# Layer B's phi on a copy: one evacuation of PSUM for the projections that need phi, and phi without a relu

## The chip, the cores and the metric

The kernel runs on one core of a Trainium2 chip. The metric is the device time of one execution in microseconds (us). The kernel before was timed in 3 runs. A profiled execution gives the trace; its times start at the beginning of its span.

Five engines work side by side, each through its own queue in order: PE (TensorE, matmuls and transposes into PSUM), PEld (its weight loads), DVE (VectorE), ACT (ScalarE), POOL (GpSimd), and SP, which issues transfers.

## What is computed

Four layers are applied one after the other to x of 2048 rows and 640 columns, in the order A, B, A, B, each as x + layer(layernorm(x)). There are 32 heads of 20 columns. Layer A is linear attention. Layer B cuts the rows into N = 4 segments of L = 512 and adds a memory, made of the keys of the segments before, to causal softmax attention inside a segment:

```python
phi = lambda t: jnp.where(t > 0, t + 1.0, jnp.exp(t))
for s in range(N):
    qs, ks, vs = q[:, :, s], k[:, :, s], v[:, :, s]
    logits = jnp.einsum("bhqd,bhkd->bhqk", qs, ks) * scale + mask
    p = _softmax(logits, axis=-1)
    a_dot = jnp.einsum("bhqk,bhkd->bhqd", p, vs)
    pq = phi(qs)
    num = jnp.einsum("bhld,bhde->bhle", pq, M)
    den = jnp.einsum("bhld,bhd->bhl", pq, z)[..., None] + 1e-6
    o = g * (num / den) + (1.0 - g) * a_dot
    outs.append(o)
    pk = phi(ks)
    M = M + jnp.einsum("bhld,bhle->bhde", pk, vs)
    z = z + jnp.einsum("bhld->bhd", pk)
```

So the queries need phi from segment 1 on (in segment 0 the memory is empty), and the keys need it up to segment 2 (nothing reads the memory after segment 3).

## The kernel before

**Projections of layer B.** `b_project` runs once for each segment. It makes v first, and then, for t = 0 to 4, a tile of 128 rows of the transposed queries and one of the transposed keys, each 128 x 512, with `proj_t`: 15 matmuls (L391) on pairs of fp16 halves into one PSUM bank of 512 fp32 columns. There are eight banks, handed out in turn by `bank`. The weights were scaled by a power of two, so a projection is p times `inv`, one value per partition.

Each such bank has up to three uses. `split_store` makes its fp16 half (L830, ScalarE) and the rest that the half leaves (L831, VectorE) in the tile `nat` of two buffers, and sends both to DRAM (`qd`, `kd`) with two transfers on SP's queue (L834, L835 for queries, L837, L838 for keys). Where phi is wanted, `phi` then takes the exponential (L428) and the relu (L430) of the same bank on ScalarE, both scaled by `inv`, into two buffers of the tag `er`, and VectorE makes min(exp, 1) + relu of them (L431). For queries that goes to `pq`, which `read_mem` multiplies with the memory (L457) once the next stretch of layer A runs; for keys to `pkT`, of one buffer, which `pk_turn` transposes on PE (L858) after the next query projection, ScalarE evacuates (L860, `pkt`) and `update` multiplies with v (L868, added to `acc` at L872 or L874).

**Attention of layer B** goes through head groups: four heads each, eight groups a segment. `stacks` loads their rows of `qd` and `kd` into `qs` and `ks` (L979, SP's queue); `row_max` makes scores (L993) and their row maxima with VectorE (L999); `max_rows` turns the maxima (L1017, L1019) and sends them into `qs` (L1022); `scores` makes the transposed scores (L1034), their exponential with ScalarE (`pe`, L1038) and masks the diagonal blocks with GpSimd (L1045); `weigh` multiplies with v (L1061); `evacuate` (L1067) and `normalize` (L1074 to L1085) write the result to `otok`.

**Order.** PE's order is written out by hand: `run` steps two streams in turn by planned costs. One is `dense` (layer A, projections, output products), the other `attend` (attention of the segment before). So while segment 1 to 3 is projected, the attention of the segment before runs, and in segment 3 of the first layer B and after it the output products follow. Inside `dense`, the projections of segment s are woven with the output of segment s - 2 and the head of layer A's next segment (`p_read`, L754 to L760). In segment 0 the projections run without attention; the second half of layer A (`a_second`, L483, `moments`) for segment 1 follows. The order of the other engines is made by the framework's scheduler, which moves instructions by their dependencies; the waits between engines are put in by it.

**Opening.** The first run through layer A also prepares all weights: it finds their maxima, the scales `scl` and their inverses `inv` (L259 to L264), and splits the weights (L269, L270). `last`, inside `opening`, ends it with `scales("B")` and the gates.

## Time and profile before

| | us |
|---|---|
| median of 3 runs | 1704.46 |
| lowest and highest | 1704.25, 1706.57 |
| profiled execution | 1704.55 |
| its span | 1702.8 |
| mean granted clock of TensorE in it | 0.992 |

The projections of queries and keys in layer B run at 299 to 337, 398 to 463, 539 to 618 and 695 to 766 us in the first layer B, and at 1129 to 1167, 1228 to 1293, 1365 to 1428 and 1498 to 1555 us in the second, for segments 0 to 3.

A row of the profile's groups gives line, engine, operation, output and inputs by the program's names, shapes and the count; behind the bars stand the busy time in us and the mean ns of one, and the idle time of that engine just before, with what ended it. In the timeline and the chain of waits each row starts with its start and its duration in us.

### The profile page before, as it was taken

The page shows a single profiled execution, that of the slowest core. Times are in us where ns is not written, and L with a number is a line of the kernel's source. Part 1 is how long each engine was busy: PE and PEld are TensorE (multiplying, and loading weights), DVE is VectorE, ACT ScalarE, POOL GpSimd, SP SyncE. Part 2 cuts the span into 40 slices and gives each one's busy share as a digit, 9 for nine tenths or more (in the row PEclk, how much of TensorE's full clock was granted, in tenths as well). Part 3 has the DMA queues.
Part 4 walks back from the last instruction along what each step waited for, and adds up shares of the span by engine and source line. Part 5 has one row for each costly group of instructions (what it writes and reads, how often), then busy time and mean ns, then how long its engine had stood idle before and what let it go on. Part 6 is the DMA issues. An engine that isn't in the chain of part 4 may idle for free.

```text
span 1702.8 us, 37843 instructions
## 1 busy us (share of the span) xinstructions
PE 1637.9 (96%) x13788; PEld 1018.6 (60%) x13788; DVE 1272.3 (75%) x4015; ACT 994.2 (58%) x1888; POOL 505.9 (30%) x1046
## 2 busy tenths in 40 slices
PE   7999979999999999999999999999999999999998
PEld 5767757554465556556566777765546545645555
DVE  7888887487887788759874465847888978878773
ACT  6666533347756746667776454333675676666673
POOL 3442222013223322333452210310322332233452
PEclk9999989999999999999999999999999999999999
DMA  6424654421322331353211303423232323323432
GB/s 218 151 75 169 223 203 152 136 98 59 111 79 69 115 118 56 128 183 95 72 56 39 117 32 125 178 94 123 70 110 89 114 83 110 102 86 111 140 103 95
DMA packets 110372, 191.00 MB, mean 112 GB/s; under 512 B 14172, under 2 KB 69596, under 8 KB 107624
## 3 DMA queue, kind: packets, MB, share of 16 engines
q1 hardware_dynamic: 97704, 142.68, 25.9%
q0 software_dynamic: 3264, 24.91, 4.1%
q10 hardware_dynamic: 9216, 20.98, 3.2%
q8 instruction: 109, 1.79, 0.4%
q14 instruction: 79, 0.65, 0.1%
HBM read 109.32 MB, written 78.64 MB: 110 GB/s over the span
## 4 chain that ended last, share of the span: by engine, by line
PE 66%; DVE 17%; ACT 9%; issue 3%; DMA 3%; POOL 2%; SPq 0%; ACTq 0%; POOLq 0%; DVEq 0%
PE ps L406 25%; PE ps L391 13%; PE ps L1061 8%; PE ps L580 4%; PE ps L1034 4%; ACT pe L1038 3%; PE ps L993 3%; PE ps L329 3%; DVE ps L999 3%; PE ps L457 2%; PE ps L1074 1%; DVE e L421 1%; DVE wmx L243 1%; DVE split L270 1%; DVE xT L334 1%
## 5 line engine op out<-in xcount | busy, mean ns | idle before, releaser
L999 DVE CUSTOM_DVE_ANT_0 ps<-ps,maskw 128x512 f32<-128x512 f32 (+3 forms) x1024 | 472.0, 518 | 28.7 <-PE ps L993 25.9
L1038 ACT ACTIVATE pe<-ps,lsc 128x512 f32<-128x512 f32 x640 | 395.4, 696 | 63.0 <-PE ps L1034 59.8
L406 PEld LDWEIGHTS <-xT 128*128 128x128 f16 x2880 | 282.2, 99 | 115.0 <-issue 6.2
L1045 POOL TENSOR_SCALAR_AFFINE_SELECT pe<-pe 128x256 f32<-128x256 f32 (+1 forms) x640 | 233.4, 372 | 350.5 <-ACT pe L1038 342.7
L406 PEld LDWEIGHTS <-oT 128*128 128x128 f16 x1920 | 184.5, 98 | 84.7 <-issue 8.3
L1061 PE MATMUL ps<-pe,v 128*32 128x512 f32 (+3 forms) x2048 | 161.6, 436 | 8.8 <-DVE oT L334 1.9
L406 PE MATMUL ps<-wm,oT 128*128 128x320 f16 x960 | 141.3, 299 | 3.8 <-DVE rs L352 2.6
L406 PE MATMUL ps<-w_Bo,oT 128*128 128x320 f16 x960 | 141.5, 299 | 3.2 <-ACT oT L333 2.0
L406 PE MATMUL ps<-w_Ak,xT 128*128 128x320 f16 x960 | 140.6, 303 | 3.1 <-DVE xT L334 1.0
L406 PE MATMUL ps<-w_Bv,xT 128*128 128x320 f16 x960 | 142.3, 303 | 0.2
L391 PE MATMUL ps<-xT,w_Bq 128*128 128x512 f16 x600 | 140.9, 379 | 1.3 <-ACT pe L1038 0.8
L999 DVE DVE_READ_ACCUMULATOR2_ANT mg<- 128x1 f32 x1024 | 142.1, 139 | 0.1
L580 PE MATMUL ps<-pk,xs 128*128 128x321 f16 (+1 forms) x960 | 140.7, 304 | 1.1 <-DVE pk L543 0.7
L391 PE MATMUL ps<-xT,w_Bk 128*128 128x512 f16 x600 | 138.5, 379 | 1.2 <-ACT pe L1038 1.2
L406 PE MATMUL ps<-w_Aq,xT 128*128 128x320 f16 x960 | 137.6, 299 | 0.1
L993 PE MATMUL ps<-ks,qs 60*128 60x512 f16 (+3 forms) x1024 | 123.5, 297 | 7.6 <-ACT pe L1038 3.5
L580 PEld LDWEIGHTS <-xs 128*128 128x128 f16 x960 | 93.9, 99 | 41.0 <-issue 1.6
L421 DVE SCALAR_TENSOR_TENSOR e<-e,r 128x320 f32<-128x320 f32 x128 | 69.6, 544 | 53.6 <-ACT r L420 53.0
L1034 PE MATMUL ps<-qs,ks 62*128 62x512 f16 (+3 forms) x1024 | 105.6, 300 | 2.1 <-ACT pe L1038 1.1
L1061 PEld LDWEIGHTS ps<-pe,v 128*32 128x32 f32 x2048 | 65.4, 109 | 68.7 <-issue 40.9
L831 DVE SCALAR_TENSOR_TENSOR nat<-ps,nat 128x512 f16<-128x512 f32 x80 | 55.2, 690 | 62.6 <-ACT nat L830 62.3
L391 PEld LDWEIGHTS <-w_Bk 128*128 128x128 f16 x600 | 57.1, 98 | 66.5 <-issue 6.4
(202 smaller groups left out, 2359.6 us busy)
## 6 DMA issues: line engine op xcount, KB each, us to landing
x<-xn ACTq DMA_DIRECT2D x48, 320.0 KB
qs<-qd SPq DMA_DIRECT2D x128, 120.0 KB
ks<-kd SPq DMA_DIRECT2D x128, 120.0 KB
xo<-x SPq DMA_DIRECT2D x48, 320.0 KB
pqi<-pqd SPq DMA_DIRECT2D x32, 320.0 KB
qd<-nat SPq DMA_DIRECT2D x40, 256.0 KB
kd<-nat SPq DMA_DIRECT2D x40, 256.0 KB
x<-in_A_x SPq DMA_DIRECT2D x16, 320.0 KB
```

The source lines that it names most:

```text
L329: nc.tensor.transpose(pt[:, (c - c0) * P:(c - c0 + 1) * P], src[:, c * P:(c + 1) * P], self.ident)
L391: nc.tensor.matmul(p, w[:, c, a, t * P:(t + 1) * P], xT[:, c, b, :], start=k == 0, stop=k == 3 * C - 1)
L406: nc.tensor.matmul(p, xT[:, c, a, i * P:(i + 1) * P], w[:, c, b, n * HN:(n + 1) * HN], start=k == 0, stop=k == 3 * C - 1)
L421: nc.vector.scalar_tensor_tensor(e, e, 1.0, r, op0=OP.min, op1=OP.add)
L580: nc.tensor.matmul(p, xs[:, i, a, c * P:(c + 1) * P], pk[i][:, b, cols], start=i == 0 and a == b, stop=i == NT - 1 and a == 1)
L831: nc.vector.scalar_tensor_tensor(nat[:, 1], p, QK_SHIFT, nat[:, 0], op0=OP.mult, op1=OP.subtract)
L993: nc.tensor.matmul(bs[par][:, a:a + n], qs[r, p, i * P:(i + 1) * P], ks[r, p, :n], start=True, stop=True)
L999: nc.vector.tensor_tensor_reduce(bs[par][:, a:a + n], bs[par][:, a:a + n], self.maskw[:, SEG - n:], 1.0, NEG, OP.add, OP.max, G["mg"][:, p ...
L1034: nc.tensor.matmul(b[:, a:a + n], ks[r, p, j * P:(j + 1) * P], qs[r, p, j * P:], start=True, stop=True)
L1038: nc.scalar.activation(e, b, AF.Exp, scale=self.lsc)
L1045: nc.gpsimd.affine_select(d, d, pattern=pat, compare_op=OP.is_ge, fill=0.0, base=0, channel_multiplier=-1)
L1061: nc.tensor.matmul(G["pv"][32 * h4:32 * h4 + 32, j * P:], v[j][:, h * E1:h * E1 + 32], G.pop((p, par, j)), start=j == 0, stop=j == 2, skip ...
```

## The change

For projections that need phi, `split_store` gets the tile that phi is to fill (`dst`: pq or pkT). ScalarE first copies the bank, scaled by `inv`, into that tile. The fp16 half, its rest and the exponential then read the copy. Since the copy is already scaled, the shift of the fp16 half becomes a value per partition, `nat_scl`, the shift times `scl`; it is made in `last`, for queries and keys. phi is then taken in place: VectorE takes min(exp, 1) in SBUF, in an instruction of its own, and then the larger of copy + 1 and that. There is no relu, and `phi` is gone. Projections that need no phi (queries of segment 0, keys of segment 3) go through `split_store` as before. In `b_project` the tile is taken ahead of `split_store`.

```diff
-    def phi(self, p, inv, dst):
-        nc, sb = self.nc, self.sb
-        n = p.shape[-1]
-        e = sb.tile([P, 512], F32, tag="er", name="e", bufs=3)[:, :n]
-        nc.scalar.activation(e, p, AF.Exp, scale=inv)
-        r = sb.tile([P, 512], F32, tag="er", name="r", bufs=3)[:, :n]
-        nc.scalar.activation(r, p, AF.Relu, scale=inv)
-        nc.vector.scalar_tensor_tensor(dst, e, 1.0, r, op0=OP.min, op1=OP.add)
...
-    def split_store(self, p, dd, t, key):
+    def split_store(self, p, dd, t, key, dst=None):
         nc = self.nc
         nat = self.bp.tile([P, 2, SEG], F16, tag="nat", name="nat", bufs=2)
-        nc.scalar.activation(nat[:, 0], p, AF.Copy, scale=QK_SHIFT)
-        nc.vector.scalar_tensor_tensor(nat[:, 1], p, QK_SHIFT, nat[:, 0], op0=OP.mult, op1=OP.subtract)
+        shift = QK_SHIFT
+        if dst is not None:
+            shift = self.nat_scl[key]
+            nc.scalar.activation(dst, p, AF.Copy, scale=self.inv["B", key])
+            p = dst
+        nc.scalar.activation(nat[:, 0], p, AF.Copy, scale=shift)
+        nc.vector.scalar_tensor_tensor(nat[:, 1], p, shift, nat[:, 0], op0=OP.mult, op1=OP.subtract)
+        if dst is not None:
+            e = self.sb.tile([P, SEG], F32, tag="er", name="e", bufs=3)
+            nc.scalar.activation(e, dst, AF.Exp)
+            nc.vector.tensor_scalar(e, e, 1.0, None, op0=OP.min)
+            nc.vector.scalar_tensor_tensor(dst, dst, 1.0, e, op0=OP.add, op1=OP.max)
...
             p = yield from self.proj_t(xT, w["q"], t)
-            self.split_store(p, st["qd"], t, "q")
+            pq = None
             if s > 0:
                 pq = sb.tile([P, SEG], F32, tag="pq", name="pq", bufs=PQ)
-                self.phi(p, self.inv["B", "q"], pq)
                 st["pq"].append(pq)
+            self.split_store(p, st["qd"], t, "q", pq)
...
             p = yield from self.proj_t(xT, w["k"], t)
-            self.split_store(p, st["kd"], t, "k")
             if s < NSEG - 1:
                 pkT = bp.tile([P, SEG], F32, tag="pkT", name="pkT", bufs=1)
-                self.phi(p, self.inv["B", "k"], pkT)
+            self.split_store(p, st["kd"], t, "k", pkT)
...
             self.scales("B")
+            self.nat_scl = {}
+            for n in "qk":
+                self.nat_scl[n] = self.cp.tile([P, 1], F32, name="nat_scl" + n)
+                self.nc.vector.tensor_scalar(self.nat_scl[n], self.scl["B", n], QK_SHIFT, None, op0=OP.mult)
```

## The prediction

> **What bounds the kernel now.** First the page: span, busy shares, and the shares by engine of the chain of waits.
>
> ```profile
> span 1702.8 us, 37843 instructions
> ...
> PE 1637.9 (96%) x13788; PEld 1018.6 (60%) x13788; DVE 1272.3 (75%) x4015; ACT 994.2 (58%) x1888; POOL 505.9 (30%) x1046
> ...
> PE 66%; DVE 17%; ACT 9%; issue 3%; DMA 3%; POOL 2%; SPq 0%; ACTq 0%; POOLq 0%; DVEq 0%
> ```
>
> TensorE sets most of the time. VectorE is 75% busy but is the link that ended last for only 17%. The profiled execution took 1704.55 us for a span of 1702.8, 0.09 above the median of 1704.46; the sum below is made on 1704.55.
>
> Then the table of busy time, in the stretches where layer B's projections run: segment 0 of the first layer B, then its segments 1 to 3, then segments 1 to 3 of the second. The columns are length, PE, PEld, DVE, ACT, POOL, clock, DMA.
>
> ```profile
> 299.00:337.00 38.00, 37.76 (x302) 18.75 (x300) 13.90 (x27) 14.00 (x25) 1.27 (x1) 1.00 0.42 137
> 398.00:463.00 65.00, 62.83 (x579) 29.73 (x579) 53.01 (x195) 50.39 (x90) 19.13 (x49) 1.00 0.29 96
> 539.00:618.40 79.40, 74.58 (x625) 39.19 (x627) 59.28 (x191) 49.68 (x90) 30.20 (x55) 1.00 0.37 119
> 695.00:765.70 70.70, 69.14 (x501) 35.76 (x500) 45.46 (x161) 45.28 (x80) 25.19 (x54) 1.00 0.48 154
> ...
> 1228.00:1293.00 65.00, 62.55 (x567) 29.53 (x571) 52.94 (x195) 50.27 (x90) 18.89 (x49) 1.00 0.29 96
> 1365.00:1428.00 63.00, 60.88 (x563) 29.12 (x566) 52.38 (x186) 48.37 (x86) 20.93 (x49) 1.00 0.31 100
> 1498.00:1555.00 57.00, 55.70 (x428) 25.20 (x427) 44.41 (x168) 40.52 (x71) 19.02 (x48) 1.00 0.30 97
> ```
>
> PE idles 0.2 us of the first stretch and 2.2, 4.8, 1.6, 2.5, 2.1 and 1.3 us of the others: 14.5 us in all. A gain here can hardly pass that. VectorE already has 53 of 65 us in segment 1, so a loss has more room.
>
> Third, one key projection of segment 0 in the timeline (start, duration, engine, line; idle before it and its releaser in brackets).
>
> ```profile
> 305.91 0.60 ACT L830 ACTIVATE nat<-ps 128x512 f16<-128x512 f32 x1 [2.64 <-PE ps L391]
> ...
> 306.54 0.69 DVE L831 SCALAR_TENSOR_TENSOR nat<-ps,nat 128x512 f16<-128x512 f32 x1 [2.54 <-ACT nat L830]
> ...
> 307.26 0.69 ACT L428 ACTIVATE e<-ps,inv_Bk 128x512 f32<-128x512 f32 x1 [0.76 <-DVE nat L831]
> ...
> 307.85 0.68 ACT L430 ACTIVATE r<-ps,inv_Bk 128x512 f32<-128x512 f32 x1
> 308.56 0.69 DVE L431 SCALAR_TENSOR_TENSOR pkT<-e,r 128x512 f32<-128x512 f32 x1 [1.33 <-ACT r L430]
> ...
> 309.35 0.63 PE L858 MATMUL ps<-ident,pkT 128*128 128x128 f32 x4 [0.24 <-PE ps L391]
> ```
>
> The exponential reads the PSUM bank that L831 reads, and starts 0.03 us after L831 ends, though it uses nothing that L831 makes. ScalarE stands idle 0.76 us for it, and the bank is held 2.6 us, until the relu ends at 308.53. Over the kernel:
>
> ```profile
> L831 DVE SCALAR_TENSOR_TENSOR nat<-ps,nat x80: 676/691/694, 303.3 to 1555.7; 128x512 f16<-128x512 f32 x80
> ...
> ACT e L428: 20.2, 28
> ```
>
> Fourth, the chain of waits by line, in segment 1 and segment 2 of the first layer, and in segments 1 and 3 of the second.
>
> ```profile
> by line: PE ps L391 38.5%; PE ps L1061 14.3%; PE ps L993 7.2%; ACT pe L1038 7.0%; PE ps L1034 5.3%; DMA pqi<-pqd 5.2%; issue 2.9%; PE ps L868 2.3%; DVE nat L831 2.1%; ACT e L428 2.1%; PE ps L1074 2.0%; ACT r L430 1.8%; ACT nat L830 1.7%; SP
> by line: PE ps L391 21.0%; PE ps L406 11.3%; PE ps L1061 9.2%; issue 6.8%; ACT pe L1038 5.5%; PE ps L1034 4.3%; DVE nat L831 4.2%; PE ps L993 3.4%; DVE pqi L754 3.2%; ACT e L428 2.7%; ACT r L430 2.6%; POOL xn L481 2.6%; PE ps L1074 2.2%; DV
> by line: PE ps L391 38.5%; PE ps L1061 14.3%; ACT pe L1038 7.0%; PE ps L993 6.9%; DMA pqi<-pqd 5.7%; PE ps L1034 5.3%; issue 2.8%; PE ps L868 2.3%; DVE nat L831 2.1%; ACT e L428 2.1%; PE ps L1074 2.0%; ACT r L430 1.8%; ACT nat L830 1.7%; DV
> by line: PE ps L391 56.9%; PE ps L1061 12.1%; PE ps L1034 8.7%; PE ps L993 7.4%; DVE ps L999 6.2%; PE ps L1074 2.3%; ACT pe L1038 1.2%; DVE pq L431 1.2%; ACT r L430 1.2%; DVE nat L831 1.2%; DVE mg L999 1.0%; issue 0.6%; DVE rc L1077 0.2%; P
> ```
>
> L831 is on the chain for 2.1% of 65, 4.2% of 79.4, 2.1% of 65 and 1.2% of 57 us: 6.7 us. That is what can be gained directly.
>
> **The change part by part.** 60 of the 80 projections need phi: queries of segments 1 to 3 and keys of segments 0 to 2, five tiles each, in two layers. The other 20 stay as they are. Prices by form:
>
> ```profile
> L556 ACT ACTIVATE pk<-e,k_scl 128x320 f16<-128x320 f32 x64 | 36.3, 568 | 37.9 <-DVE e L421 37.6
> L487 ACT ACTIVATE xs<-xh 128x640 f16<-128x640 f32 x32 | 22.8, 732 | 0.0
> ...
> L543 DVE SCALAR_TENSOR_TENSOR pk<-e,k_scl,pk 128x320 f16<-128x320 f32 x64 | 45.2, 711 | 11.0 <-ACT pk L556 9.4
> ...
> L570 DVE TENSOR_SCALAR e<-e 128x320 f32<-128x320 f32 x64 | 26.8, 419 | 1.2
> ...
> L270 DVE SCALAR_TENSOR_TENSOR w_Ak<-stage,scl_Ak,w_Ak 128x320 f16<-128x320 f32 x10 | 4.8, 545 | 0.0
> L270 DVE SCALAR_TENSOR_TENSOR w_Aq<-stage,scl_Aq,w_Aq 128x640 f16<-128x640 f32 x5 | 4.1, 876 | 0.0
> ```
>
> ScalarE keeps three instructions. The relu becomes a scaled copy of the same form: 0.69. The fp16 half now reads SBUF with a scale per partition. L556 is that at 320 columns, 0.57; at 512 it lies between the relu's 0.69 (such a scale, but PSUM) and L487's 0.73 (SBUF, 640 columns, a constant): I take 0.72. The exponential loses its scale operand and reads SBUF: between L830's 0.60 and L487's 0.73, near the first, 0.63. The three make 2.04 against 0.60 + 0.69 + 0.69 = 1.98: **+0.06 a unit**.
>
> VectorE goes from two instructions to three. The fp16 rest has both inputs in SBUF and a scale per partition: L270 has 545 ns for 320 and 876 for 640 columns, 1.03 a column, so 0.74 for 512, against 0.69: +0.05. The last one keeps its form, 0.69. The min is new; the nearest row is the tensor-scalar L570 with 320 columns. Its min/median/max, and those of L543, which makes the rest of layer A's keys:
>
> ```profile
> L570 DVE TENSOR_SCALAR e<-e x64: 302/326/3072, 64.4 to 1084.7; 128x320 f32<-128x320 f32 x64
> L543 DVE SCALAR_TENSOR_TENSOR pk<-e,k_scl,pk x64: 539/556/2239, 25.3 to 1054.6; 128x320 f16<-128x320 f32 x64
> ```
>
> At half of 1.03 ns a column, 192 more columns on the median of 0.326 give 0.43; at the whole, 0.52. I take 0.43, since 0.326 for 320 columns is well under L270's 0.545. So VectorE gets **+0.48 a unit**, 29 us in all. The Trainium skill ("VectorE: DVE Perf Modes", section on the perf-mode tier table) lets an fp32 tensor-scalar in SBUF run at twice the rate, and L570 agrees; without it the sum would be 0.6 us higher.
>
> **Added waiting beside GpSimd.** L831 reads PSUM, and in 80 runs never took more than 694 ns. L543 and L570, all in SBUF, reach 2239 and 3072; their means, 711 and 419, lie 155 and 93 ns above the medians. If the new rest and the min pay that too, it is another 0.25 a unit. The lower end is nothing. The Trainium skill ("SBUF — State Buffer", section "Who interferes with whom") says that a VectorE instruction with two SBUF inputs contends with a GpSimd instruction that reads SBUF, and that a two-port one locks it out; it speaks against this change. By that rule each of the 120 instructions could wait out one mask of layer B, 0.37 by the row below (an estimate): 44 us in place of 15, and 3.5 us on top of my sum. The trace agrees in kind.
>
> ```profile
> L1045 POOL TENSOR_SCALAR_AFFINE_SELECT pe<-pe 128x256 f32<-128x256 f32 (+1 forms) x640 | 233.4, 372 | 350.5 <-ACT pe L1038 342.7
> ```
>
> How much of this ends on the path? From the page, 17% on the chain over 75% busy: 0.23 us for each us of VectorE work, as an upper end. In the segment 1 rows VectorE shows hardly more than 2.1% over 82% busy: 0.03, the lower end. I take 0.12 for the stretches without a place of their own.
>
> - *After segment 0* VectorE paces the second half of layer A; that stretch's row of the chain begins so:
>
> ```profile
> by line: DVE ps L999 21.5%; PE ps L406 16.7%; DVE xn L483 5.9%; DVE st L348 5.6%; issue 5.3%; PE ps L1061 4.5%; ACT pe L1038 3.8%; POOL rs L353 3.6%; DVE oT L334 3.3%; DVE mg L999 3.3%; DVE xT L334 3.2%; PE ps L993 3.0%; DVE pqi L754 2.5%;
> ```
>
> The last key tile falls into it (337 to 398 in the first layer): +0.48 in each layer, **+1.0**.
> - *Segment 2 of the first layer* has a run, 601.8 to 614.5, where VectorE alone is the chain:
>
> ```profile
> by line: DVE pqi L754 18.4%; DVE nat L831 14.1%; DVE mem L739 12.2%; DVE rca L757 10.1%; DVE pkT L431 9.8%; issue 8.3%; POOL rs L371 7.1%; DVE rca L759 6.3%; DVE rca L758 6.2%; PE ps L858 3.9%; DVE oT L334 2.5%; DVE acc L874 1.9%; DVE nb L3
> ...
> 605.38 0.67 DVE pkT L431
> ...
> 610.73 0.06 DVE pq L431
> ...
> 613.74 0.70 DVE pkT L431
> ...
> 614.49 0.55 PE ps L858 x3
> ```
>
> (The row by line is of 601 to 615.) Three units pass through it; the transposes L858 wait for the end: 3 x 0.48 = **+1.4**.
> - *The other 47 units* of segments 1 to 3: 22.6 us x 0.12 = **+2.7**, between 0.7 and 5.2. Behind a late min on VectorE stand row maxima (L999), and behind those the banks that PE wants for L993.
> - *GpSimd*: 60 x 0.25 x 0.12 = **+1.8**, between 0 and 3.5. **ScalarE**: 50 x 0.06, most of it hidden beside PE: **+0.4**, at most 3.
> - *The removed wait*: 6.7 us of the chain, less the 2.0 of the run above (14.1% of 14 us, which stay), is 4.7. What comes late next is ScalarE's own queue (L1038 has 5.5 to 7.0% of these stretches), so I take half: **-2.4**, between 0 and -4.7.
> - *The bank* is free after 0.69 instead of 2.6 us. PE waited for its readers very little (us, times, longest):
>
> ```profile
> PE ps L1061 <- ACT r L430: 0.9, 3, 0.6
> ...
> PE ps L391 <- DVE nat L831: 0.3, 1, 0.3
> ```
>
> **-0.6**, between 0 and -1.2.
> - *Keys of segment 0*: pkT is done at 309.25, PE asks for it at 309.11. With the change: 305.91 + 0.69 + 0.72, then 0.74, 0.43 and 0.69 on VectorE, is 309.18. Nothing gained; if the min and what follows it don't overlap, 0.3 late, eight times: **0**, up to +2.4.
> - *Stores* of the fp16 halves leave 0.8 us later on SP's queue. Their number is unchanged; a head group's loads come after its projections, and only the first of a segment could feel it: **0**, up to +1. pq and pkT are now taken by the copy, ahead of the split, but their last readers stand earlier in PE's order: 0.
> - *Two more column scales* in the opening, on VectorE, each like the scale below on the chain, in a run that VectorE paces: **+0.2**.
>
> ```profile
> 231.72 0.07 DVE scl_Bo L264
> ```
>
> Sum: 1.0 + 1.4 + 2.7 + 1.8 + 0.4 - 2.4 - 0.6 + 0.2 = +4.5, so 1704.55 + 4.5 = **1709.0 us**. The lower ends, with the named places hidden, make 1699; the upper ends 1722.
>
> **Rivals.** *ScalarE's queue paces the projections, and the change is faster.* For it: 20.2 us of waits of L428 for L831, up to 6.7 of them on the chain, the ACT entries beside them. Against: ScalarE's work doesn't shrink. Then all 6.7 and the 1.2 of banks go, 2.4 are added at the two named places: -5.5, **1699.0**. It decides if L1038 moves up by what L428 no longer waits.
>
> *All is hidden.* VectorE's idle 12 of 65 us swallow 7 us more, gains are taken by the next wait; only +1.0 after segment 0 remains: **1705.5**.
>
> *VectorE becomes the bound of segments 1 and 2.* Ten units x 0.73 lift 53 to 60 of 65 us, and it must wait for PE's banks in between. From the point where its queue no longer empties within a slot, half of 50 x 0.73 = 36 us shows: +18, **1722**. Against: the low shares of VectorE on these chains.
>
> *The change doesn't do what it says*: if ScalarE's order puts other work between the copy and the exponential, phi comes later and the waits move to L858; that is the +2.4 above, inside the range.
>
> **How the numbers follow.** Forecast 0.47, faster 0.24, all hidden 0.17, VectorE bound 0.12. About 0.2% (3.4 us) is what a measurement can tell from no change. The forecast falls within it with 0.05, the hidden case with 0.13, its rest on both sides alike. Slower 0.42 + 0.02 + 0.12 = 0.56, within 0.05 + 0.13 = 0.18, faster 0.24 + 0.02 = 0.26. The range 1698 to 1722 leaves out half of the VectorE rival and the tails of the others; the forecast's own is 1705 to 1716.
>
> **What would show it.** Right: the exponential no longer waits for the fp16 rest; a min near 0.43 with a tail, the rest near 0.74 with a tail; VectorE's busy time up by 30 to 45 us; the stretch at 600 to 615 longer by 1 to 2 us; PE idle in segments 1 and 2 not smaller. Wrong: PE's 14.5 us of idle shrink by 5 or more (the first rival), VectorE at 90% of segment 1 with waits of L993 for L999 (the third), or the order on ScalarE and VectorE so different that another stage moves by more than these terms.

## The result, and the profile after

| | kernel before | changed kernel |
|---|---|---|
| median of the runs, us | 1704.92 (6 runs, 1700.92 to 1706.57) | 1718.57 (6 runs, 1716.15 to 1719.28) |
| ratio to before, 95% interval | | 1.0079 [1.0069, 1.0090] |
| profiled execution, us (span) | 1704.55 (1702.8) | 1718.51 (1716.8) |

The change makes the kernel 13.5 us slower by the ratio. The page of the changed kernel:

```profile
span 1716.8 us, 37906 instructions
...
PE 1648.4 (96%) x13788; PEld 1019.6 (59%) x13788; DVE 1301.5 (76%) x4077; ACT 998.2 (58%) x1888; POOL 516.1 (30%) x1046
...
PE 65%; DVE 18%; ACT 8%; DMA 4%; issue 3%; POOL 2%; SPq 0%; ACTq 0%; POOLq 0%; DVEq 0%
```

VectorE has 29.2 us more to do, ScalarE 4.0, GpSimd 10.2 with the same instructions. PE's shares hardly move, so the page alone doesn't show where the time went. The 13788 matmuls stand in the same order in both kernels, but for three swapped pairs of neighbours, and the start of each can be compared one by one; the delay grows in the projections of layer B. The table of busy time over the same pieces of PE's work (columns as before) of the changed kernel:

```profile
300.20:338.00 37.80, 37.37 (x274) 18.22 (x276) 15.77 (x31) 14.07 (x24) 1.27 (x1) 1.00 0.42 138
398.90:465.60 66.70, 63.85 (x561) 29.38 (x562) 57.19 (x204) 50.72 (x89) 21.10 (x49) 1.00 0.28 90
542.10:625.10 83.00, 76.29 (x621) 39.30 (x618) 64.88 (x200) 50.92 (x90) 32.33 (x55) 0.98 0.35 111
701.60:773.30 71.70, 69.42 (x502) 35.61 (x501) 48.17 (x166) 45.76 (x80) 25.94 (x54) 1.00 0.48 151
...
1235.60:1301.90 66.30, 64.34 (x562) 29.60 (x563) 57.16 (x204) 50.40 (x89) 21.28 (x49) 1.00 0.29 91
1373.90:1439.10 65.20, 62.24 (x550) 29.11 (x552) 57.01 (x195) 48.26 (x85) 22.29 (x49) 1.00 0.30 93
1509.00:1567.20 58.20, 57.02 (x430) 25.38 (x429) 47.41 (x173) 41.14 (x71) 19.81 (x48) 1.00 0.29 92
```

Segment 0 is 0.4 us longer by the starts of its matmuls, and 0.6 in the second layer (its row above is 37.80 us and not longer than before's 38.00, because the two windows don't end at the same matmul); what it loses is made up again by the end of the stretch that follows. Segments 1 to 3 are longer by 1.7, 3.6, 1.0 in the first layer and 1.3, 2.2, 1.2 us in the second: 11.0 of the 14.0 us between the two profiled executions. Of the others, 1.0 us arises ahead of 121 us, where the change adds nothing, and 1.7 us is a stretch of half clock at 1659.7. VectorE's busy time in segment 1 goes from 53.0 to 57.2 us. Over the six rows of segments 1 to 3 PE's idle time grows by 3.5 us and its busy time by 7.5; 1.7 of that is a stretch of half clock in segment 2. What makes the rest of the busy time longer this view doesn't tell: the ends of matmuls are modelled in it.

The same key projection of segment 0, in the timeline:

```profile
306.93 0.69 ACT L825 ACTIVATE pkT<-ps,inv_Bk 128x512 f32<-128x512 f32 x1 [2.64 <-PE ps L391]
...
307.64 0.72 ACT L827 ACTIVATE nat<-pkT,nat_sclk 128x512 f16<-128x512 f32 x1
308.27 0.61 ACT L831 ACTIVATE e<-pkT 128x512 f32<-128x512 f32 x1
...
308.40 0.75 DVE L828 SCALAR_TENSOR_TENSOR nat<-pkT,nat_sclk,nat 128x512 f16<-128x512 f32 x1 [3.39 <-ACT nat L827]
309.07 0.42 DVE L832 TENSOR_SCALAR e<-e 128x512 f32<-128x512 f32 x1
...
309.52 0.69 DVE L833 SCALAR_TENSOR_TENSOR pkT<-pkT,e 128x512 f32<-128x512 f32 x1
```

The exponential no longer waits for the rest: copy, half and exponential run through. But the fp16 rest (L828) now starts 1.47 us after the bank was ready, where L831 started after 0.63. And when it ends, the exponential is there already, so VectorE does rest, min and phi in one go. How often that is so is seen in the groups by form: duration, mean, then idle time ahead of them and what ended it. First before, then after:

```profile
L831 DVE SCALAR_TENSOR_TENSOR nat<-ps,nat 128x512 f16<-128x512 f32 x80 | 55.2, 690 | 62.6 <-ACT nat L830 62.3
...
L431 DVE SCALAR_TENSOR_TENSOR pq<-e,r 128x512 f32<-128x512 f32 x30 | 21.1, 704 | 24.1 <-ACT r L430 23.7
L431 DVE SCALAR_TENSOR_TENSOR pkT<-e,r 128x512 f32<-128x512 f32 x30 | 20.7, 690 | 13.8 <-ACT r L430 13.4
```

```profile
L832 DVE TENSOR_SCALAR e<-e 128x512 f32<-128x512 f32 x60 | 28.0, 467 | 0.0
...
L828 DVE SCALAR_TENSOR_TENSOR nat<-pkT,nat_sclk,nat 128x512 f16<-128x512 f32 x30 | 24.4, 813 | 14.9 <-ACT nat L827 14.4 <-DMA qs<-qd 0.3
...
L828 DVE SCALAR_TENSOR_TENSOR nat<-pq,nat_sclq,nat 128x512 f16<-128x512 f32 x30 | 23.5, 785 | 25.1 <-ACT nat L827 24.9 <-DMA qs<-qd 0.2
...
L833 DVE SCALAR_TENSOR_TENSOR pkT<-pkT,e 128x512 f32<-128x512 f32 x30 | 21.5, 716 | 0.4
L833 DVE SCALAR_TENSOR_TENSOR pq<-pq,e 128x512 f32<-128x512 f32 x30 | 20.9, 696 | 0.6
```

Before, VectorE stood idle 37.9 us ahead of phi's last instruction, until the relu was done, and what else it did between the rest and phi was mostly the attention's row maxima (197 other instructions over the 60 units, by the order of its queue). After, it idles 1.0 us there, and 54 other instructions stand in between, all behind the min. So the wait inside the unit has gone, with the hole in which a min could have lain.

What that does to the attention is seen in the first query projection of segment 1. Before, then after:

```profile
403.39 1.29 ACT L1038 ACTIVATE pe<-ps,lsc 128x512 f32<-128x512 f32 x2
...
403.57 0.69 DVE L831 SCALAR_TENSOR_TENSOR nat<-ps,nat 128x512 f16<-128x512 f32 x1 [0.39 <-ACT nat L830]
...
404.17 0.69 DVE L999 CUSTOM_DVE_ANT_0 ps<-ps,maskw 128x512 f32<-128x512 f32 x1
...
404.54 0.73 ACT L428 ACTIVATE e<-ps,inv_Bq 128x512 f32<-128x512 f32 x1
```

```profile
404.28 0.72 ACT L1039 ACTIVATE pe<-ps,lsc 128x512 f32<-128x512 f32 x1
...
404.85 0.75 ACT L827 ACTIVATE nat<-pq,nat_sclq 128x512 f16<-128x512 f32 x1
...
405.46 0.66 ACT L831 ACTIVATE e<-pq 128x512 f32<-128x512 f32 x1
...
405.98 0.72 ACT L1039 ACTIVATE pe<-ps,lsc 128x512 f32<-128x512 f32 x1
...
407.23 0.63 PE L1062 MATMUL ps<-pe,v 128*32 128x256 f32 x6 [0.63 <-POOL pe L1046]
```

Before, two exponentials of the attention (pe) and a row maximum (L999) ran between half and phi's exponential. After, one pe still runs between the copy and the half, none between the half and the exponential, and the next one stands behind all three instructions of the unit; PE idles 0.63 us for its mask. PE's waits that grew most (us, times, longest), of the changed kernel:

```profile
PE ps L994 <- DVE mg L1000: 5.8, 11, 1.4
PE ps L994 <- ACT pe L1039: 4.8, 19, 0.6
PE ps L1062 <- POOL pe L1046: 4.4, 9, 0.6
PE ps L329 <- POOL pqi L751: 4.1, 1, 4.1
```

The same four were 3.0, 3.5, 1.7 and 1.1 before: 9.8 us more of waiting for row maxima, exponentials, masks and one pair of the memory's queries, which GpSimd multiplies with a reciprocal (L751). Others shrank. These waits must not be taken for the whole cause. A run below, e2_new_no_min, has the copy but no min and costs 1.4 us, and its first three are as long as in the changed kernel (its lines are one lower):

```profile
PE ps L993 <- DVE mg L999: 5.8, 9, 1.4
PE ps L993 <- ACT pe L1038: 5.2, 20, 0.6
PE ps L1061 <- POOL pe L1045: 4.4, 10, 0.8
```

Only the last of the four is much shorter there (0.8). It is a single place, in segment 2 of the first layer:

```profile
603.04 1.53 POOL L371 TENSOR_TENSOR rs<-rs,mhalf 128x4 f32<-128x4 f32 x1 [2.08 <-DVE rs L370]
...
604.61 0.16 DVE L373 SCALAR_TENSOR_TENSOR nb<-mv,rs 128x4 f32<-128x4 f32 x1 [0.92 <-POOL rs L371]
...
605.50 0.34 DVE L750 RECIPROCAL rca<-rca 128x32 f32<-128x32 f32 x1
...
605.93 3.48 POOL L751 TENSOR_TENSOR pqi<-pqi,rca 128x640 f32<-128x640 f32 x2 [1.35 <-DVE rca L749]
...
606.78 1.50 DVE L828 SCALAR_TENSOR_TENSOR nat<-pkT,nat_sclk,nat 128x512 f16<-128x512 f32 x1
...
607.79 0.55 PE L329 MATMUL ps<-ident,pqi 128*128 128x128 f32 x3 [4.07 <-POOL pqi L751]
...
608.17 3.79 PE L391 MATMUL ps<-xT,w_Bq 128*128 128x512 f16 x9
608.20 1.49 DVE L832 TENSOR_SCALAR e<-e 128x512 f32<-128x512 f32 x1
```

The same place before:

```profile
599.10 0.30 DVE L759 RECIPROCAL rca<-rca 128x32 f32<-128x32 f32 x1
...
599.48 1.27 POOL L760 TENSOR_TENSOR pqi<-pqi,rca 128x640 f32<-128x640 f32 x1 [1.75 <-DVE rs L370]
...
601.76 0.16 DVE L373 SCALAR_TENSOR_TENSOR nb<-mv,rs 128x4 f32<-128x4 f32 x1 [1.63 <-POOL rs L371]
```

It is the order of VectorE's queue that makes most of this wait. Before, the reciprocal stood ahead of L373, which belongs to a layernorm; in the changed kernel it stands behind it, and L373 waits 0.92 us for GpSimd's L371. So the reciprocal is taken 6.4 us later, in a kernel that was 4.0 us late up to there, and PE's wait grows by 3.0 us. The rest and the min take 1.50 and 1.49 here in place of 0.75 and 0.42, beside two GpSimd multiplications that take 1.81 and 1.71 (their mean is 1.33): they overlap, and each is longer than its median. But PE waits for the first of the two, which begins 0.85 us ahead of the rest and is only 0.53 us over its median of 1.27. And e11_rest_psum below, whose rest never takes more than 0.69, has the same wait of 4.1 us. PE is idle for 4.07 us, and its next nine matmuls run at half the clock, as the table of busy time says for these 3.4 us (the third number from the end is the clock):

```profile
608.35:611.75 3.40, 3.40 (x9) 1.29 (x8) 3.40 (x7) 0.49 (x1) 1.23 (x2) 0.50 0.55 174
611.80:615.00 3.20, 3.20 (x19) 1.85 (x18) 2.38 (x6) 1.87 (x4) 1.05 (x1) 1.00 0.02 5
```

### The profile page after: what moved, and what is told of

It is laid out like the page before. It is cut to its first block, busy times and chain, and to the rows that moved or that the text cites. A ratio compares the mean times of both kernels' runs of the same rounds, so it can differ in the third digit from the quotient of the medians.

```text
span 1716.8 us, 37906 instructions
## 1 busy us (share of the span) xinstructions
PE 1648.4 (96%) x13788; PEld 1019.6 (59%) x13788; DVE 1301.5 (76%) x4077; ACT 998.2 (58%) x1888; POOL 516.1 (30%) x1046
## 4 chain that ended last, share of the span: by engine, by line
PE 65%; DVE 18%; ACT 8%; DMA 4%; issue 3%; POOL 2%; SPq 0%; ACTq 0%; POOLq 0%; DVEq 0%
PE ps L406 26%; PE ps L391 12%; PE ps L1062 7%; PE ps L571 4%; PE ps L1035 4%; PE ps L994 3%; DVE ps L1000 3%; PE ps L329 3%; ACT pe L1039 3%; PE ps L448 2%; PE ps L1075 1%; DVE e L421 1%; DVE split L270 1%; DVE wmx L243 1%; DMA pqi<-pqd 1%
## 5 line engine op out<-in xcount | busy, mean ns | idle before, releaser
L1000 DVE CUSTOM_DVE_ANT_0 ps<-ps,maskw 128x512 f32<-128x512 f32 (+3 forms) x1024 | 473.2, 520 | 30.8 <-PE ps L994 27.9
L1046 POOL TENSOR_SCALAR_AFFINE_SELECT pe<-pe 128x256 f32<-128x256 f32 (+1 forms) x640 | 240.9, 385 | 338.1 <-ACT pe L1039 334.3
L1000 DVE DVE_READ_ACCUMULATOR2_ANT mg<- 128x1 f32 x1024 | 145.1, 142 | 0.0
L994 PE MATMUL ps<-ks,qs 60*128 60x512 f16 (+3 forms) x1024 | 126.4, 297 | 12.1 <-DVE mg L1000 5.8
L994 PEld LDWEIGHTS <-qs 60*128 60x128 f16 x1024 | 50.5, 94 | 79.2 <-issue 54.3
```

The lines of the kernel that those rows point to most:

```text
L994: nc.tensor.matmul(bs[par][:, a:a + n], qs[r, p, i * P:(i + 1) * P], ks[r, p, :n], start=True, stop=True)
L1000: nc.vector.tensor_tensor_reduce(bs[par][:, a:a + n], bs[par][:, a:a + n], self.maskw[:, SEG - n:], 1.0, NEG, OP.add, OP.max, G["mg"][:, p ...
L1046: nc.gpsimd.affine_select(d, d, pattern=pat, compare_op=OP.is_ge, fill=0.0, base=0, channel_multiplier=-1)
```

## The experiments

The working theory after the result was that the min on VectorE costs the time; the rivals were ScalarE's order (phi's instructions in front of the attention's exponentials), the copy ahead of the fp16 half (half, rest and stores late), and VectorE contending with GpSimd in SBUF. Each run below is named by its label and compared with the kernel before in runs on the same chip; microseconds are the ratio less one times 1704.5. e2, e8 and e13 leave out the bound of the exponential in phi.

| run | min | rest done | phi done | median | ratio, 95% interval | us | more clock lost | us at equal clock |
|---|---|---|---|---|---|---|---|---|
| kernel before | no | 1.41 | 3.67 | 1704.92 | | | | |
| e4_new_phi_psum | yes | 1.41 | 3.86 | 1706.13 | 1.0008 [0.9998, 1.0019] | +1.4 | +0.4 | +1.1 |
| e1_old_min | yes | 1.46 | 3.91 | 1708.25 | 1.0015 [1.0007, 1.0024] | +2.6 | -0.5 | +3.0 |
| e10_split_first | yes | 1.44 | 4.68 | 1713.40 | 1.0049 [1.0037, 1.0061] | +8.4 | +5.0 | +4.8 |
| e12_copy_first_psum | yes | 1.94 | 3.35 | 1711.71 | 1.0047 [1.0034, 1.0060] | +8.0 | +3.7 | +5.3 |
| e11_rest_psum | yes | 2.46 | 3.75 | 1718.98 | 1.0078 [1.0060, 1.0095] | +13.3 | +5.7 | +9.2 |
| changed kernel | yes | 2.60 | 3.86 | 1718.57 | 1.0079 [1.0069, 1.0090] | +13.5 | +4.2 | +10.5 |
| e7_wait_back | yes | 2.61 | 4.94 | 1717.55 | 1.0077 [1.0064, 1.0090] | +13.1 | +0.2 | +13.0 |
| e13_min_behind_phi | behind phi | 2.67 | 3.59 | 1714.77 | 1.0047 [1.0032, 1.0062] | +8.0 | +0.8 | +7.4 |
| e2_new_no_min | no | 2.64 | 3.59 | 1704.69 | 1.0008 [0.9998, 1.0018] | +1.4 | -1.5 | +2.5 |
| e8_wait_no_min | no | 2.41 | 4.12 | 1710.08 | 1.0035 [1.0022, 1.0047] | +6.0 | +4.5 | +2.8 |
| e3_copy_old_phi | no | 2.60 | 3.58 | 1714.69 | 1.0057 [1.0045, 1.0069] | +9.7 | -1.7 | +10.9 |
| e5_old_rest_last | no | 2.51 | 3.11 | 1712.11 | 1.0041 [1.0029, 1.0053] | +7.0 | +1.0 | +6.3 |
| e9_keys_no_relu | keys | | | 1703.11 | 0.9989 [0.9980, 0.9999] | -1.9 | +0.5 | -2.3 |

"Rest done" and "phi done" are the median times in us, over the 60 units with phi in each trace, from the end of the projection's last matmul to the end of the fp16 rest and of phi.

The last two columns hold a rival that no run was made for: the granted clock. "More clock lost" is a run's time times one less its mean granted clock, on average, less the same of the kernel before on its chip (of all its 68 runs for the changed kernel). "At equal clock" takes off 0.72 us for each us of that, the slope found within kernels (last section), and is an estimate. The clock isn't independent of the edits for certain, since a stall may set off a stretch of half clock (the one at 608 follows a PE idle for 4.07 us). But it doesn't follow the loss either: e7 loses 13.1 us with hardly more lost clock, e8 6.0 with 4.5.

**The min alone, without the copy.** e1_old_min puts a separate min into the kernel before:

```diff
         nc.scalar.activation(r, p, AF.Relu, scale=inv)
+        nc.vector.tensor_scalar(e, e, 1.0, None, op0=OP.min)
         nc.vector.scalar_tensor_tensor(dst, e, 1.0, r, op0=OP.min, op1=OP.add)
```

> The kernel before with one thing added: VectorE takes min(exp, 1) in an instruction of its own, 60 times, ahead of L431, which is left as it was. ScalarE's order and work are those of before. Theory 1 (the added VectorE work is what costs: 60 x 0.42 us, which delays the row maxima and the banks that PE wants for L993): 8 to 12 us slower than before, most of the 13.7. Theory 2 (ScalarE's queue: without the wait for the bank no exponential of the attention gets in between the copy, the half and phi's exponential, so the exponentials come later): 0 to 3 us slower. Theory 3 (the run around GpSimd's pow and p_read at 600 us and the half clock after it): near 0 to 2.

e4_new_phi_psum takes the new formula for phi, but half, rest and exponential read the bank as before, and the copy stands in the relu's place:

```diff
-        r = sb.tile([P, 512], F32, tag="er", name="r", bufs=3)[:, :n]
-        nc.scalar.activation(r, p, AF.Relu, scale=inv)
-        nc.vector.scalar_tensor_tensor(dst, e, 1.0, r, op0=OP.min, op1=OP.add)
+        nc.scalar.activation(dst, p, AF.Copy, scale=inv)
+        nc.vector.tensor_scalar(e, e, 1.0, None, op0=OP.min)
+        nc.vector.scalar_tensor_tensor(dst, dst, 1.0, e, op0=OP.add, op1=OP.max)
```

> The new phi alone: fp16 half, its rest and the exponential are taken from PSUM as before, the copy takes the relu's place on ScalarE, and phi is the larger of copy + 1 and min(exp, 1), with three instructions on VectorE. ScalarE's order is that of before, with 44 exponentials of the attention inside. Theory 2: +2 to +4 us, like the added min. Theory 1: +8 or more.

Measured: +2.6 and +1.4 us for 28 us of added VectorE work, as by the second reading or a little less. So neither the min by itself nor the new formula is what costs 13.5. The groups by form of e1_old_min show where the min went:

```profile
L431 DVE TENSOR_SCALAR e<-e 128x512 f32<-128x512 f32 x60 | 28.4, 474 | 20.7 <-ACT e L428 20.5
...
L432 DVE SCALAR_TENSOR_TENSOR pq<-e,r 128x512 f32<-128x512 f32 x30 | 21.6, 719 | 2.7 <-ACT r L430 2.3
L432 DVE SCALAR_TENSOR_TENSOR pkT<-e,r 128x512 f32<-128x512 f32 x30 | 20.9, 696 | 1.8 <-ACT r L430 1.2
```

The idle time inside the unit goes from 37.9 to 25.2 us: 12.7 of the 28.4 lie in time in which VectorE waited anyway. In both runs 139 other instructions of VectorE stand between the rest and the min.

**The copy without the min.** e2_new_no_min is the changed kernel without L832, so the exponential has no bound:

> The changed kernel with the min left out, so phi is the larger of x + 1 and exp x (that is not phi for x over 0). VectorE is back at two instructions, ScalarE's order is that of the changed kernel. Theory 1: 2 to 5 us over before. Theory 2: 9 to 13 us over before, little less than the changed kernel. Theory 3: 5 to 7 less than the changed kernel if the stall at 600 us goes, else the same.

+1.4 us, below both readings. The copy, with everything reading it, costs hardly anything as long as VectorE has two instructions; a min that costs 1.4 to 2.6 without the copy costs 12.1 with it. The two together cost far more than the sum of each. At equal clock the step from no min to min behind the copy is 8.0 us and not 12.1, still far above 1.1 to 3.0. So the question became what the copy does to the price of the min.

**ScalarE's order.** In the changed kernel no attention exponential stands between half and phi's exponential; before, 44 do over the 60 units. e7_wait_back makes the exponential wait for the fp16 rest again, and 46 stand between; e8_wait_no_min is that without the min:

```diff
-        nc.vector.scalar_tensor_tensor(nat[:, 1], p, shift, nat[:, 0], op0=OP.mult, op1=OP.subtract)
+        rest = nc.vector.scalar_tensor_tensor(nat[:, 1], p, shift, nat[:, 0], op0=OP.mult, op1=OP.subtract)
...
-            nc.scalar.activation(e, dst, AF.Exp)
+            ex = nc.scalar.activation(e, dst, AF.Exp)
+            self.tc.add_manual_dep(ex.ins, rest.ins.name, ...)
```

> The changed kernel with one wait put back: phi's exponential waits for the fp16 rest on VectorE, as it did before over the bank, though it doesn't need it. All work is that of the changed kernel, the min too. In the order made for it 46 exponentials of the attention stand between the halves and phi's exponentials; before had 44, the changed kernel has none. Theory 2 (the three instructions of a projection in one block on ScalarE hold up the attention's exponentials): 2 to 5 us over before, near the old kernel with an added min (+2.6), so 8 to 11 faster than the changed kernel. Theory 1 (VectorE's work): the min is still there, 10 us or more over before.

> The same wait put back and the min left out (phi is then the larger of x + 1 and exp x). Theory 2 with the min as a second, smaller cost: -2 to +2 us against before. Theory 1 alone: like the changed kernel without the min, +1 to +2 by its time, +5 in the projections' stretches.

+13.1 and +6.0. The order that the wait had given doesn't bring the time back, so ScalarE's order isn't the cause by itself. e8 lies outside both readings by its time. Without the min, putting the wait back costs 6.0 - 1.4 = 4.6 us; with the min it changes nothing that can be measured (13.1 against 13.5). But this pair doesn't price the wait: e8 lost 6.0 us more of clock than e2, and at equal clock they differ by 0.3. With the min, e7 is 2.5 above the changed kernel at equal clock.

**One part late, nothing added.** e5_old_rest_last has the instructions of the kernel before, but in the order half, exponential, relu, rest; the rest is 1.10 us later and phi 0.56 earlier:

> The kernel before with one order changed: the fp16 half, the exponential and the relu stand together on ScalarE, and only then VectorE makes the fp16 rest, so ScalarE never waits for VectorE over the bank. Work of both engines as before. Theory 1: 0 to 3 us faster than before, since only the wait is gone. Theory 2 (the wait let attention's exponentials pass): 3 to 8 us slower than before.

e3_copy_old_phi has the copy and phi from a relu on ScalarE: one more ScalarE instruction than the run without a min, and the same two on VectorE:

```diff
             nc.scalar.activation(e, dst, AF.Exp)
-            nc.vector.tensor_scalar(e, e, 1.0, None, op0=OP.min)
-            nc.vector.scalar_tensor_tensor(dst, dst, 1.0, e, op0=OP.add, op1=OP.max)
+            r = self.sb.tile([P, SEG], F32, tag="er", name="r", bufs=3)
+            nc.scalar.activation(r, dst, AF.Relu)
+            nc.vector.scalar_tensor_tensor(dst, e, 1.0, r, op0=OP.min, op1=OP.add)
```

> The copy alone: the bank is copied once and all else reads the copy, but phi is the old one, min(exp, 1) + relu, with the relu taken by ScalarE from the copy. VectorE two instructions, ScalarE four, 60 x 0.6 us more than the changed kernel. Theory 1: 2 to 6 us over before. Theory 2: more than the changed kernel, 15 to 22 over before, since each unit keeps ScalarE's queue 0.6 longer.

+7.0 and +9.7. The first costs 7.0 us with no work added at all: an order alone can cost that much. The second lies between its two readings, 8.3 us above e2_new_no_min for 28 us of ScalarE work (0.30 for each us), at a clock that differs by 0.2 us. Its rest and phi are done as early as in e2 (2.60 and 3.58 against 2.64 and 3.59), so it isn't a longer unit that is paid here, and it isn't VectorE alone: once the copy stands ahead, added time on either engine is.

**Late, or contended?** The rest of the changed kernel has both inputs in SBUF and was seen at up to 1.50 us beside GpSimd. Three runs take half and rest from the bank: ahead of the copy (e10), the rest alone (e11), both but behind the copy (e12). The lines ahead of the exponential:

```diff
 e10_split_first
+        nc.scalar.activation(nat[:, 0], p, AF.Copy, scale=QK_SHIFT)
+        nc.vector.scalar_tensor_tensor(nat[:, 1], p, QK_SHIFT, nat[:, 0], op0=OP.mult, op1=OP.subtract)
+        if dst is not None:
+            nc.scalar.activation(dst, p, AF.Copy, scale=self.inv["B", key])
 e11_rest_psum
+            nc.scalar.activation(dst, p, AF.Copy, scale=self.inv["B", key])
+        nc.scalar.activation(nat[:, 0], p if dst is None else dst, AF.Copy, scale=shift)
+        nc.vector.scalar_tensor_tensor(nat[:, 1], p, QK_SHIFT, nat[:, 0], op0=OP.mult, op1=OP.subtract)
 e12_copy_first_psum
+            nc.scalar.activation(dst, p, AF.Copy, scale=self.inv["B", key])
+        nc.scalar.activation(nat[:, 0], p, AF.Copy, scale=QK_SHIFT)
+        nc.vector.scalar_tensor_tensor(nat[:, 1], p, QK_SHIFT, nat[:, 0], op0=OP.mult, op1=OP.subtract)
```

> The change's phi with its copy, exponential from the copy, min and larger-of, but the fp16 half and the fp16 rest are taken straight from the PSUM bank, ahead of the copy, as in the kernel before. So VectorE keeps the min (0.42 us) in every unit and the same number of instructions as the changed kernel; the half is ready 0.7 us earlier than there and the rest has one SBUF input, not two. If the late fp16 half and rest cost the time (stores, the loads behind them on SP, and what stands behind on VectorE), 1706 to 1708. If the two SBUF inputs beside GpSimd cost it, the same 1706 to 1708. If it is the number of VectorE instructions and phi's own length that cost it, 1714 to 1719, since phi is ready even later here than in the changed kernel.

> The changed kernel in which only the fp16 rest reads the PSUM bank again (0.69 in every run, one SBUF input); copy first and half from the copy, so half and rest are as late as in the changed kernel by some 0.7 us. If lateness costs the time, it stays at 1715 to 1719. If the contention of the rest's two SBUF inputs with GpSimd costs it, 1709 to 1712, and no rest in the trace much over 0.70.

> The copy first, but the half and the rest both from the PSUM bank with a constant scale (0.60 and 0.69), the exponential from the copy: half and rest late by the copy alone (0.7 us), no SBUF input of the split but the half itself. If lateness alone costs the time, 1714 to 1718; if it is the slower and contended SBUF reads of half and rest, 1707 to 1710; if both, in between, and the difference to the run with the split first is the price of the lateness alone.

e11_rest_psum: +13.3, all of the loss within some 3 us of uncertainty, with a rest that was never slowed (the line's durations, min/median/max in ns):

```profile
L827 DVE SCALAR_TENSOR_TENSOR nat<-ps,nat x80: 627/692/693, 301.8 to 1561.7; 128x512 f16<-128x512 f32 x80
```

(That is its profiled execution, at 1710.66 the shortest of six; the longest took 1720.47.) So the two SBUF inputs of the rest are not the main cause; the rival of contention falls for the rest (the min's own contention is in all these runs). e12 costs 8.0, where half and rest are late by the copy alone. The late copy alone had been put at 1714 to 1718 and slower reads alone at 1707 to 1710; it lies in between. The difference to e10 was to price the lateness alone; it is -0.4, but phi is done 1.33 us earlier in e12, so it doesn't. In e10 two of the three readings expected 1706 to 1708, and it came near the third, phi's own length: half and rest are in time there, and VectorE does have its hole ahead of the min,

```profile
L829 DVE TENSOR_SCALAR e<-e 128x512 f32<-128x512 f32 x60 | 25.5, 425 | 41.7 <-ACT e L828 41.2
```

but phi is done 0.82 us later than in e4_new_phi_psum, whose instructions differ in that the exponential reads the bank and the copy comes behind it. The difference is 8.4 - 1.4 = 7.0 us, 3.7 at equal clock. PE waits 4.4 us for pkT, against 2.2 before. So a late phi is paid, too, though the queues' orders differ as well: 60 exponentials of the attention stand between half and exponential here, 44 in e4.

**The min's time, or what waits for phi?** e13_min_behind_phi leaves the min in VectorE's queue but takes it off phi's path:

```diff
-            nc.vector.tensor_scalar(e, e, 1.0, None, op0=OP.min)
             nc.vector.scalar_tensor_tensor(dst, dst, 1.0, e, op0=OP.add, op1=OP.max)
+            nc.vector.tensor_scalar(e, e, 1.0, None, op0=OP.min)
```

> The changed kernel with the min moved behind the last instruction of phi, where nothing needs its result: VectorE does the same 60 mins of 0.42 us, but phi is ready as in the run without a min. It leaves out the bound of the exponential for positive entries (phi is wrong there). If the price of the min is that it takes VectorE's time in front of the attention's row maxima, it stays near the changed kernel: 1713 to 1719. If the price is that phi is ready 0.25 us later and what waits for phi is late, it falls to that of the run without a min: 1703 to 1707.

The median of 1714.77 lies in the range of the first reading; by the ratio it is +8.0, 1712.5, between the two and nearer the first. The min's time on VectorE costs 8.0 - 1.4 = 6.6 us even where nothing waits for it, 0.23 for each of its 29 us; the other 13.5 - 8.0 = 5.5 came with phi 0.27 us later. Each of these differences is uncertain by about 3 us, from the intervals of the two runs it is made of, and at equal clock they are 4.9 (0.17 for each us) and 3.1. That the second is the price of a late phi isn't shown: of PE's waits, the one for L751 at 607 is 1.9 us here in place of 4.1, and no half clock follows it; the wait for row maxima (L994 for L1000) is 5.4 against 5.8.

**A version that beats both.** e9_keys_no_relu starts from the kernel before, leaves the query side alone and takes the relu out for keys only, without a copy: phi - 1 is the larger of x and min(exp, 1) - 1, and the 1 is added by the evacuation that follows the transposes anyway.

```diff
+                nc.scalar.activation(e, p, AF.Exp, scale=inv)
+                nc.vector.tensor_scalar(e, e, 1.0, -1.0, op0=OP.min, op1=OP.add)
+                nc.vector.scalar_tensor_tensor(pkT, p, inv, e, op0=OP.mult, op1=OP.max)
...
-            nc.scalar.activation(pk, pt, AF.Copy)
+            nc.scalar.activation(pk, pt, AF.Copy, bias=1.0)
```

> A version that may beat both: the kernel before, for keys without the relu: VectorE takes min(exp, 1) - 1 and then the larger of the scaled bank and that, which is phi - 1, and the evacuation after the transposes adds the 1. ScalarE loses 30 x 0.69 us, VectorE gains 30 x 0.42. If ScalarE's blocks are what costs, 1 to 4 us faster than before; if VectorE's work is, 1 to 4 slower.

Ratio 0.9989 [0.9980, 0.9999]: 1.9 us, hardly more than what can be measured. ScalarE loses 30 instructions (994.2 to 979.5 us), VectorE gets 9.2 us more. So without a copy ahead, a min on VectorE in place of a relu on ScalarE can pay a little.

Left open: a min on GpSimd wasn't tried. And e2_new_no_min and e5_old_rest_last have the rest equally late (2.64 and 2.51), yet one costs 1.4 and the other 7.0 (2.5 and 6.3 at equal clock). They differ in when the bank is free (after the copy, or only when the rest is done) and in phi's formula; no run tells these apart. What lowers the granted clock in some kernels and not in others is open, too. The framework orders each kernel's queues anew, so every run moves more than its edit.

## Why the prediction was right or wrong

The direction and the range were right: 1709.0 was forecast, 1698 to 1722 given, 1718.57 came. The size of the sum was not: +4.5 against +13.5. The result lies above 1705 to 1716, the forecast's own range. That it is inside the whole range is in part luck, for the upper end comes from all terms at their worst together and from the rival that VectorE becomes the bound, which isn't what happened. The parts, regrouped as the runs price them:

| part of the sum | forecast | runs | at equal clock |
|---|---|---|---|
| copy ahead, half and rest from it, the wait left in (rest 0.5, its contention 0.9, ScalarE 0.4, scales 0.2) | +2.0 | +6.0 (e8) | +2.8 |
| the removed wait and the bank | -3.0 | -4.6 (e2 less e8) | -0.3 |
| the min's time on VectorE (its nine tenths of 1.0 + 1.4 + 2.7, half of the GpSimd term) | +5.5 | +6.6 (e13 less e2) | +4.9 |
| phi later by the min | 0 | +5.5 (changed kernel less e13) | +3.1 |
| lower granted clock | 0 | in the rows above | +3.0 |
| sum | +4.5 | +13.5 | +13.5 |

The two right columns add up by the way they are made, each row from one run less another. Each row is uncertain by some 3 us in the first of them. Firm is the price of the min behind the copy, 12.1 us or 8.0 at equal clock, against 1.4 to 2.6 without the copy; how it splits is not.

*The prices of the instructions held.* Copy 0.69, half 0.72, exponential 0.61, rest 0.75, min 0.42, phi 0.69 in the timeline above, against 0.69, 0.72, 0.63, 0.74, 0.43 and 0.69. Rest and min have the tails that the forecast took from L543 and L570: maxima 1498 ns, means 785 to 813 and 467 against 0.75 and 0.42 at the median, about 0.1 a unit and not 0.25. VectorE's busy time rose by 29.2, just under the 30 to 45 named, and PE's idle time in segments 1 and 2 did not shrink. GpSimd's share of the contention came on its own side: its masks of 256 columns rose from a mean of 419 to 430 ns.

*The removed wait* was taken at -2.4, and its gain isn't borne out. e2 less e8 gives -4.6, bank included, but the lower lost clock of e2 makes up nearly all of it. The exponential did stop waiting; no run shows that PE gained by it. The first rival, that ScalarE's queue paces the projections, had counted this gain in full, and no gain came.

*Stores: 0, up to +1*, and ScalarE +0.4, "most of it hidden beside PE". The sum had looked at ScalarE's busy time, which hardly grows, and not at the order: the same work with the rest 1.1 us late costs 7.0 (e5). And ScalarE's time isn't hidden once the copy stands ahead: 28 us of it cost 8.3 (e3). For the changed kernel itself the copy's row above, +6.0, is half clock in large part; at equal clock it is 2.8, near the forecast of 2.0.

*Keys of segment 0: nothing gained.* Right for the unit shown: 3.27 us from the bank to phi forecast, 3.28 in the row above (306.93 to 310.21). Of the five units of each layer's segment 0 two are like it, and three have phi 0.2 to 0.6 us later than before; the stretch grew by 0.4 and 0.6 us. The +1.0 for the second half of layer A behind it didn't show: by 398 and 1228 us the delay is within 0.3 us of what it was at 299 and 1129. And the same sum was not made for segments 1 to 3, where VectorE has other work: there phi came 0.14 us later by the medians, at 4.00 in place of 3.86, and the forecast has no term for it. This is the largest part that the sum put at nothing: e13 leaves 5.5 us for it, 3.1 at equal clock, part of it the wait for L751 and not phi.

*The weight of VectorE's time.* The 0.12 us for each us was taken between 0.03 and 0.23. It fits the order of before, where the runs give 2.6 / 28.4 = 0.09 and 1.4 / 27.4 = 0.05, and is too small for the order after, 0.23 or, at equal clock, 0.17. The share of the chain was read from a trace in which VectorE still had 37.9 us of idle time inside these very units; the change itself takes them away. That this is why the weight rose fits the traces and isn't shown by itself: e10 keeps 41.7 us of idle time ahead of its min and still costs 8.4. The named places behaved in kind: the stretch from 601 on is where the most is lost, 3.6 us in that segment in place of 1.4, of which 1.7 is half clock; but what lost it is the order around the reciprocal, not three mins in a row.

*The rival that VectorE becomes the bound* was off in its mechanism: VectorE is at 57.2 of 66.7 us in segment 1, 86% and not 90, and PE's waits are scattered, not those of a full queue.

The Trainium skill ("SBUF — State Buffer", "Who interferes with whom") spoke against the change, and its 3.5 us on top would have come nearer. But e11_rest_psum takes the rest out of that rule's reach and stays at +13.3: the trace agrees with the rule at single places (1.50 and 1.49 above), and the loss doesn't hang on it for the rest. The Trainium skill ("VectorE: DVE Perf Modes", "Rules for kernel authors") offers a copy to SBUF first where there will be many operations on a matmul's output. The runs disagree here: the rest takes 690 ns from PSUM and 785 to 813 from the copy, and of the kernels that compute phi in full the best three (e9, e4, e1) take half and rest straight from the bank, though e10 does so too and costs 8.4.

## What to carry to other kernels

A wait inside a short chain of two engines is also a hole in which other work runs: before removing it, look at what lies in the hole (here row maxima and exponentials of the attention), and what the new instruction would find there. An engine's weight on the path, read from the chain before, holds for the order before; price an added instruction in the order that the change will make. Readers that end later don't tell the price by themselves: the rest some 1.1 to 1.2 us late cost 7.0 us in one order and 1.4 in another. And before a wait that grew is called the cause, look whether it is as long in a run that lost nothing, and whether the runs compared had the same granted clock.

## What the runs showed of the hardware

The granted clock drops to half for 3.4 us at a time, or for 6.8. The profiled execution before has six such stretches, two of them of 6.8 us, 13.7 us of clock lost; the one after has nine, one of them of 6.8, 17.1 us lost: 3.4 us of the 14.0 between the two. Each 3.4 us cost PE up to 1.7 us. The clock makes most of the spread from run to run: over the 98 runs of the experiments and of the changed kernel, a run whose mean clock says 1 us more lost took 0.72 us longer than its kernel's mean, with a correlation of 0.91. The mean clock of the changed kernel is 0.9910 over its 6 runs against 0.9934 over 68 of the kernel before; times 1718, that is 4.1 us of clock, and with the slope of 0.72 about 3 of the 13.5 us. Of the nine stretches after, the one at 608 follows a PE idle for 4.07 us, as the Trainium skill ("TensorE: Matmul & The Clock Gate", "HAM oscillation — how this bites in real kernels") has it for waits past some 3.4 us; the trace agrees with its number there. One more, at 222.6, begins inside a wait of 5.5 us. The other seven begin where PE had been idle for only 1.3 to 2.7 of the 3.4 us before. Of the two that make the difference, 608 stands behind the wait that the change made, and 1659.7 beside none. So a stall may cost more than its length, and a difference of 1 to 2 us between two single executions says nothing.
